# Query projection in two 64-row halves, runs of four or eight heads at a time, in a fused attention and MLP kernel

## The chip, the cores and the metric

The kernel runs on one core of one Trainium2 chip. The metric is the device time of one execution in microseconds (us), given as the median of several runs with its lowest and highest. Profiles are single executions; their span is a few us off the median, which matters only where it is said.

## The reference, cut to what matters

```python
xn = layernorm(x)                                    # S=2048 rows, D=576 columns, bf16
# A: attention over the last W=512 keys of the cache, 32 query heads, 16 key heads, Dh=128
q = (xn @ wq).reshape(1, S, 32, 128)                 # wq: 576 x 4096
k, v = last W keys of k_cache, v_cache, each repeated for two query heads
s = (softmax(q @ k.T * Dh**-0.5) @ v).reshape(1, S, 4096) @ wo
# B: an MLP block of the same input
h  = gelu(layernorm(xn) @ w1)                        # 576 x 576
hs = (quarters of h shifted by +1, -1, +2, -2 rows) @ w2
x1 = xn + hs
g  = silu(x1 + gelu(layernorm(x1) @ w3) @ w4)        # inner width 4608
out = x + s * g
```

## The kernel before

The 2048 rows are four blocks of 512 (numbered 0 to 3). A block goes through 32 attention *units*, one per head. A unit is: the q projection of the next head, four score matmuls (one per 128 keys) each followed by an exp on ACT, and the sixteen output matmuls of the head before, whose result DVE divides by the softmax sums into a buffer `o`; SP then transposes `o` by DMA. Work of other stages (the first half of B, the product with wo of the block before) is put between these as filler. Block 0 also has to load and transpose all keys and load V, wq, w1 and wo.

```python
P, QB, NDC = 128, 512, 5            # 576 = 4 * 128 + 64: five passes, the last one half zeros
ps_sc = pool("ps_sc", 3, PSUM)      # score banks
ps_pq = pool("ps_pq", 2, PSUM)      # q banks
ps_po = pool("ps_po", 2, PSUM)      # output banks
o_pool = pool("o_pool", 4)

def load_wq(j, eng=None):                      # weights of four heads
    ...
    eng.dma_start(out=w[:, 0:NF, :], in_=A_wq[0:NF * P, ...])
    eng.dma_start(out=w[0:DR, NF, :], in_=A_wq[NF * P:D, ...])      # the 64 rows left

def late(ap, fn):                              # a load that may start only once `ap` is there
    g = nc.gpsimd.tensor_copy(out=gate[:, :], in_=ap)
    with tc.issue_after(g.ins):
        fn()

def stage_q(u):
    ...
    psq = ps_pq.tile([P, QB], FP32, name="psq", tag="pq")
    for kc in range(NDC):
        nc.tensor.matmul(psq[:, :], lhsT=w[:, kc, hh * Dh:(hh + 1) * Dh], rhs=xT_b[qb % 2][:, kc, :],
                         start=(kc == 0), stop=(kc == NDC - 1))
    ...                                        # DVE (block 0) or ACT copies psq to qT

def stage_v(u, t0):                            # two of the four row tiles of a head
    ...
    with tc.high_priority(offset=HP):
        nc.vector.reciprocal(out=ri, in_=po[:, :, Dh])
        nc.vector.tensor_tensor(out=o[:, t0:t0 + 2, :], in0=po[:, :, 0:Dh], in1=..., op=ALU.mult)

def stage_t(u):
    oT_t[u] = oT = oT_pool.tile([P, TB, P], BF16, name="oT")
    nc.sync.dma_start(out=oT[:], in_=o_t.pop(u)[:].rearrange("p a b -> p (a b)"), transpose=True)

# loads of block 0, by unit                    (all of these on the POOL queue)
at(2, lambda: late(pT_t[2]..., load_w1))
for i in range(8):
    at(4 + 3 * i, lambda i=i: late(pT_t[4 + 3 * i]..., lambda: load_wo(i)))
...
with tc.manual_schedule(engines={SP, POOL, PE}):   # DVE and ACT are ordered by priority
    for u in ...:
        for i in range(4):
            stage_s(u, i)
            if i == 0:
                stage_q(u + 1)                     # one head's q in every unit
            elif i < 3:
                stage_v(u - 1, 2 * (i - 1))
            ...                                    # a third of the unit's filler
        stage_t(u - 1)
```

## Time and profile before

| | |
|---|---|
| median of 3 runs | 853.12 us (850.93 to 855.52) |
| span of the profiled run | 847.5 us |
| from the first exp to block 1 (block 0) | 103.1 us |
| blocks 1, 2, 3 | 133.7, 134.3, 136.8 us |
| product with wo of block 3, then the MLP | 32.9 us, then 293.7 us |

A stage time here runs from the first exp of a block to the first exp of the next, read from the trace.

The second view is the last line of the transposed outputs' own view, the time from the issue of a transpose to its landing:

```profile
DMA to landing us min/median/max: 2.4/3.2/9.8
```

### The profile page before, as it was taken

How to read it: one execution, taken by the hardware profiler on the slowest of the kernel's cores; microseconds unless marked ns; L12 is line 12 of the kernel's file. 1: busy time of each engine (PE TensorE's matmuls, PEld its weight loads, DVE VectorE, ACT ScalarE, POOL GpSimd, SP SyncE). 2: the span in 40 equal slices, each digit the busy share in tenths (PEclk: the TensorE clock that was granted, in tenths of full speed). 3: DMA queues.
4: the chain of work that ended last, by engine and by line, in shares of the span. 5: the costliest groups of instructions: out<-in, count | busy, mean ns of one | idle time of the engine just before them, and what ended most of it. 6: DMA issues, size and time to landing. Idle time of an engine off the chain costs nothing.

```text
span 847.5 us, 19375 instructions
## 1 busy us (share of the span) xinstructions
PE 826.8 (98%) x7896; PEld 485.0 (57%) x7980; DVE 427.7 (50%) x1351; ACT 460.9 (54%) x825; POOL 76.9 (9%) x134
## 2 busy tenths in 40 slices
PE   8999899999999999999999999999999999999996
PEld 5665555665564565565566565455555555555555
DVE  5778841267751166762154884052247537635324
ACT  5776763598793388784379874132333333334610
POOL 3441200310010111010001100000000000000000
PEclk9999999999999999999999999999999999999999
DMA  7996751473372174363048336992003301310101
GB/s 181 234 234 159 157 97 41 117 125 91 87 136 43 41 130 99 91 126 82 19 82 164 70 79 105 307 342 47 2 2 74 99 2 43 69 64 15 44 15 46
DMA packets 139983, 83.94 MB, mean 99 GB/s; under 512 B 106944, under 2 KB 133248, under 8 KB 139888
## 3 DMA queue, kind: packets, MB, share of 16 engines
q1 hardware_dynamic: 130048, 53.01, 30.6%
q0 software_dynamic: 8448, 28.15, 11.8%
q10 hardware_dynamic: 1392, 1.48, 0.5%
q8 instruction: 64, 1.05, 0.5%
q14 instruction: 31, 0.25, 0.1%
HBM read 49.17 MB, written 9.44 MB: 69 GB/s over the span
## 4 chain that ended last, share of the span: by engine, by line

## 5 line engine op out<-in xcount | busy, mean ns | idle before, releaser
L367 ACT ACTIVATE pT<-sc 128x512 bf16<-128x512 f32 x512 | 290.3, 596 | 103.5 <-PE sc L365 91.4
L365 PE MATMUL sc<-qT,kT 128*128 128x512 bf16 x493 | 175.1, 378 | 1.3 <-DVE qT L355 0.6
L382 PEld LDWEIGHTS <-pT 128*128 128x128 bf16 x2048 | 139.5, 98 | 52.9 <-DVE o L387 2.5
L382 PE MATMUL po<-v_sb,pT 128*128 128x129 bf16 x2048 | 161.4, 220 | 3.2 <-DVE o L387 2.0
L350 PE MATMUL psq<-xT_b,wq_b 128*128 128x512 bf16 x603 | 151.9, 379 | 2.5 <-DMA xT_b<-xn_b 0.4
L386 DVE RECIPROCAL ri_b<-po 128x2 f32<-128x2 f32 x256 | 43.0, 168 | 189.3 <-PE po L382 185.3
L731 PE MATMUL ph<-xT_b,w_s 64*128 64x512 bf16 x976 | 127.1, 376 | 2.3 <-DVE fence L721 2.1
L768 PE MATMUL pm<-w_s,h 64*128 64x512 bf16 x864 | 122.2, 377 | 0.9 <-DVE fence L721 0.9
L406 PE MATMUL pswo<-wo_sb,oT 128*128 128x512 bf16 x497 | 114.2, 379 | 0.8
L387 DVE TENSOR_TENSOR o<-po,ri_b 128x256 bf16<-128x256 f32 x256 | 107.9, 422 | 10.7 <-DMA oT<-o 4.3
L749 ACT ACTIVATE h<-ph 128x512 bf16<-128x512 f32 x67 | 39.4, 597 | 133.9 <-PE ph L731 133.9
L350 PEld LDWEIGHTS <-wq_b 128*128 128x128 bf16 x640 | 62.4, 98 | 74.4 <-issue 2.2
L768 PEld LDWEIGHTS <-h 64*128 64x128 bf16 x1728 | 70.8, 94 | 56.7 <-issue 1.6
L406 PEld LDWEIGHTS <-oT 128*128 128x128 bf16 x1024 | 64.9, 98 | 55.2
L768 PE MATMUL pr<-w_s,h 64*128 64x64 bf16 x864 | 90.2, 189 | 0.2 <-ACT h L749 0.2
L731 PEld LDWEIGHTS <-w_s 64*128 64x128 bf16 x1152 | 57.3, 94 | 51.0 <-issue 2.8
L357 ACT ACTIVATE qT<-psq 128x512 bf16<-128x512 f32 x96 | 57.4, 598 | 28.1 <-PE psq L350 26.7
L747 DVE COPY hx<-ph 128x512 f32<-128x512 f32 x55 | 38.0, 692 | 67.8 <-PE ph L731 67.8
L365 PEld LDWEIGHTS <-kT 128*128 128x128 bf16 x512 | 47.4, 97 | 28.4 <-DVE qT L355 1.2
L227 POOL DMA_DIRECT2D wq_b<-in_A_wq_dram x30 | 23.4, 780 | 314.4 <-PE psq L350 295.4
L721 DVE TENSOR_SCALAR fence<-ph,ph 1x1 f32<-1x1 f32 x61 | 12.6, 206 | 53.9 <-PE ph L731 53.4
L749 ACT ACTIVATE h<-hx 128x512 bf16<-128x512 f32 x55 | 34.6, 630 | 8.5 <-DVE hx L747 7.0
(114 smaller groups left out, 641.3 us busy)
## 6 DMA issues: line engine op xcount, KB each, us to landing
wq_b<-in_A_wq_dram POOLq DMA_DIRECT2D x30, 512.0 KB, 5.3
w_s<-in_B_w_dram SPq DMA_DIRECT2D x9, 576.0 KB, 7.0
wo_sb<-in_A_wo_dram POOLq DMA_DIRECT2D x8, 576.0 KB, 5.0
w_s<-in_B_w_dram SPq DMA_DIRECT2D x9, 512.0 KB, 7.9
x_dram<-x SPq DMA_DIRECT2D x4, 576.0 KB, 3.5
x<-x_dram SPq DMA_DIRECT2D x4, 576.0 KB, 5.1
s_b<-s_dram SPq DMA_DIRECT2D x4, 576.0 KB, 5.4
x_b<-in_A_x_dram SPq DMA_DIRECT2D x4, 576.0 KB, 6.6
```

Of the source, the lines that this page charges most:

```text
L350: nc.tensor.matmul(psq[:, :], lhsT=w[:, kc, hh * Dh:(hh + 1) * Dh], rhs=xT_b[qb % 2][:, kc, :], start=(kc == 0), stop=(kc == NDC - 1))
L357: nc.scalar.activation(out=qT[:, :], in_=psq[:, :], func=ACT.Copy)
L365: nc.tensor.matmul(sc[:, :], lhsT=kT[:, g, kc * P:(kc + 1) * P], rhs=qT_t[u][:, :], start=True, stop=True)
L367: nc.scalar.activation(out=pT[:, :], in_=sc[:, :], func=ACT.Exp, scale=SCALE)
L382: nc.tensor.matmul(po[:, j, :], lhsT=pTs[kc][:, tt * P:(tt + 1) * P], rhs=v_sb[:, g, kc, 0:Dh + 1], start=(kc == 0), stop=(kc == KCH - 1))
L386: nc.vector.reciprocal(out=ri, in_=po[:, :, Dh])
L387: nc.vector.tensor_tensor(out=o[:, t0:t0 + 2, :], in0=po[:, :, 0:Dh], in1=ri.unsqueeze(2).to_broadcast([P, 2, Dh]), op=ALU.mult)
L406: nc.tensor.matmul(ps, lhsT=oT_t[qb * Hq + h][:, tt, :], rhs=wo_sb[:, h, lo:hi], start=(h == 0), stop=(h == Hq - 1))
L731: nc.tensor.matmul(ps[i][:, :], lhsT=lhsT, rhs=xT[half, kc, :], start=first, stop=last, skip_group_check=True)
L747: nc.vector.tensor_copy(out=src[:, :], in_=ps[i][:, :])
L749: nc.scalar.activation(out=h3[:, :], in_=src[:, :], func=ACT.Gelu_apprx_tanh)
L768: nc.tensor.matmul(out, lhsT=h3_t[b, fc][half, tt * P:(tt + 1) * P], rhs=w4_s[fc // WS][half, fc % WS, lo:hi], start=key not in started, s ...
```

## The change

The intent is to take the zeros out of q. A 64-row PE tile does half the rows of a matmul, and two such tiles, the upper and the lower half of the array, work side by side. For two heads the 576 rows are 18 half passes in 9 slots instead of 10 full passes. Since changing between full and half tiles costs time (some 0.2 us there and back in these traces), four heads (in block 0) or eight (in blocks 1 to 3) are done in one run. That needs banks: a run borrows score and output banks, chosen by who needs them next. DVE and ACT now run in a hand-made order, in which layernorm and gelu come as small pieces, each with an estimated time, placed when a credit of TensorE time has built up. Block 0's weight loads are moved to other units.

```diff
+        def stage_qs(u0, n):
+            ...
+            X, Y, Z = (ps_pq, "pq"), (ps_po, "po"), (ps_sc, "sc")
+            banks = [X, Y] if u0 == 0 else [Z, X] if n == 4 else [X, Y, Z, X]
+            for u2 in range(u0, u0 + n, 4):
+                for u in (u2, u2 + 2):
+                    ps = [... two banks ...]
+                    q_half(xT, u, ps, [(kc, ((0, LO), (1, HI))) for kc in range(NDC)], True)
+                    nc.vector.tensor_scalar(out=f[:, :], in0=ps[0][0:1, 0:1], scalar1=ps[1][0:1, 0:1], ...)  # fence
+                for u, ps in pairs:
+                    q_half(xT, u, ps, [(kc, ((1, LO), (0, HI))) for kc in range(NF)], False)
+                    nc.scalar.activation(out=qT_t[u][:, :], in_=ps[0][:, :], func=ACT.Copy)
+                    nc.vector.tensor_copy(out=qT_t[u + 1][:, :], in_=ps[1][:, :])
+        def quarter(us):                        # called after each quarter of a unit
+            clock["credit"] = min(clock["credit"] + us, 1.2)
+            while clock["credit"] > 0.25:       # put one more small piece on DVE
+                ...
@@ load_wq: the tail rows go to both halves of the array
-            eng.dma_start(out=w[0:DR, NF, :], in_=A_wq[NF * P:D, c0:c0 + 4 * Dh])
+            for half in (LO, HI):
+                eng.dma_start(out=w[half, NF, :], in_=A_wq[NF * P:D, c0:c0 + 4 * Dh])
@@ pools and loads
-        o_pool = pool("o_pool", 4)
+        o_pool = pool("o_pool", 5)
-        at(2, lambda: late(pT_t[2][0][0:1, 0:1], load_w1))
+        at(13, lambda: late(pT_t[13][0][0:1, 0:1], load_w1))
-            at(4 + 3 * i, lambda i=i: late(pT_t[4 + 3 * i][0][0:1, 0:1], lambda: load_wo(i)))
+            at(9 + 3 * i, lambda i=i: late(pT_t[9 + 3 * i][0][0:1, 0:1], lambda: load_wo(i)))
-            at(4 * (j - 1) - 1, lambda j=j: load_wq(j))
+            at(4 * (j - 2) + 1 if j < 10 else 8 * (j // 2 - 1) + 1 + j % 2, lambda j=j: load_wq(j))
@@ the order; us is the TensorE time that an atom of filler is said to take
-        def pe(u, atoms):
+        def pe(u, atoms, us=0.216):
-                pe(o2 + 3, b2_rem(bb))
+                pe(u + 3, b2_rem(bb))
-        with tc.manual_schedule(engines={SP, POOL, PE}):
+        with tc.manual_schedule(engines={SP, POOL, PE, DVE, ACTE}):
+                if u % (4 if u < Hq else 8) == 0 and 0 < u < U:
+                    stage_qs(u, 4 if u < Hq else 8)
-                        if u + 1 < U:
-                            stage_q(u + 1)
@@ also: Newton's inverse square root in four steps instead of one; layernorm's tail
@@ columns written twice; x loaded straight into the layernorm buffer; (cut)
```

## The prediction

> **What bounds the kernel now.** I read the page first, then busy time by stretch, then what TensorE waited for, then single units of the attention loop in order of time. The page's first section says who is full:
>
> ```profile
> PE 826.8 (98%) x7896; PEld 485.0 (57%) x7980; DVE 427.7 (50%) x1351; ACT 460.9 (54%) x825; POOL 76.9 (9%) x134
> ```
>
> By stretch (attention block 0, then block 1, then the start of the MLP; columns are length, then busy us and count of each engine):
>
> ```profile
> 12.50:113.50 101.00, 97.88 (x829) 61.26 (x845) 79.23 (x256) 73.53 (x131) 30.90 (x52) 1.00 0.85 180
> 113.50:248.00 134.50, 133.44 (x1110) 79.74 (x1129) 65.19 (x225) 92.76 (x172) 17.40 (x30) 1.00 0.45 97
> ...
> 554.00:660.00 106.00, 103.69 (x1296) 56.90 (x1294) 50.50 (x153) 37.04 (x61) 0.00 (x0) 1.00 0.32 84
> ```
>
> TensorE (first number after the length) is full in every stage. Block 0 is where ACT (fourth, 73.5 of 101) and DVE (third, 79.2) come nearest to it and the DMA engines are busy 0.85 of the time. So a change pays only where it shortens TensorE's own instruction stream or removes one of its waits. The waits, one list before 554 us and one after it (total us, times, longest):
>
> ```profile
> PE po L382 <- DVE o L387: 2.0, 1, 2.0
> ...
> PE ph L731 <- DVE fence L721: 2.1, 2, 1.0
> PE pm L768 <- DVE fence L721: 0.9, 1, 0.9
> ```
>
> The first is at 103 us: an attention output waits in DVE for a buffer that a slow DMA transpose holds. The other three sit in the MLP at 567, 648 and 720 us. At each, DVE is in the middle of the eleven small operations of one Newton inverse square root, 0.2 us apart, all ahead of the fence that TensorE needs. Together the waits of any size are only some 7 us; the rest of the time is instructions.
>
> One attention unit (one head of one block) without filler work, in order of time:
>
> ```profile
> 108.66 0.38 PE L365 MATMUL sc<-qT,kT 128*128 128x512 bf16 x1
> 108.88 0.63 PE L382 MATMUL po<-v_sb,pT 128*128 128x129 bf16 x8
> 109.34 0.59 PE L365 MATMUL sc<-qT,kT 128*128 128x512 bf16 x2
> 109.99 1.03 PE L350 MATMUL psq<-xT_b,wq_b 128*128 128x512 bf16 x4
> 110.85 0.38 PE L365 MATMUL sc<-qT,kT 128*128 128x512 bf16 x1
> 111.07 0.63 PE L382 MATMUL po<-v_sb,pT 128*128 128x129 bf16 x8
> 111.54 0.38 PE L365 MATMUL sc<-qT,kT 128*128 128x512 bf16 x1
> ```
>
> Start to start, a 512-column matmul costs 0.216 us (110.85 to 111.07; its 0.38 is latency) and eight 129-column ones 0.47 (0.059 each). The unit takes 111.54 - 108.66 = 2.88 us = 4 scores x 0.216 + 5 q x 0.216 (one q record is missing from the trace) + 16 x 0.059. The q projection is 1.08 of it: 576 rows done as five passes of 128, the last half zeros.
>
> **What the Trainium skill says.** "TensorE: Matmul & The Clock Gate", section "Wait — 56ns, not 53.3ns?", gives 215.7 ns start to start for 512 columns at full clock; the trace agrees (0.216). "TensorEngine Tiling (Array Packing)", section "Key Properties": two 64-row tiles work in parallel, but changing the tiling mode drains TensorE; and its "Gotcha 1: PSUM Pressure" says that different row tiles must not write one PSUM bank at once and software has to see to it, which is what the fences are for. The MLP of the kernel before already runs this way and shows both the rate and the drain:
>
> ```profile
> 551.81 2.03 PE L406 MATMUL pswr<-wo_sb,oT 128*128 128x64 bf16 x64
> 553.77 1.04 PE L731 MATMUL ph<-xT_b,w_s 64*128 64x512 bf16 x8
> 554.65 0.38 PE L731 MATMUL ph<-xT_b,w3r_s 64*128 64x512 bf16 x2
> 554.86 0.81 PE L731 MATMUL pr<-xT_b,w_s 64*128 64x512 bf16 x6
> ```
> ```profile
> 804.45 1.04 PE L731 MATMUL ph<-xT_b,w_s 64*128 64x512 bf16 x8
> 805.43 0.39 PE L931 MATMUL pm<-w_s,h 128*128 128x512 bf16 x1
> ```
>
> A pair of 64-row matmuls takes the slot of one (554.65 to 554.86). Into the mode: the last 64-column matmul starts at 551.81 + 2.03 - 0.19 = 553.65 and the next comes 0.12 later instead of 0.03, so 0.10 lost (0.01 more on the first slot). Out of it: the last pair starts at 804.45 + 1.04 - 0.38 = 805.11 and the next comes after 0.32 instead of 0.20, so 0.12 (0.01 more). A round trip is about 0.23 us. "ScalarE: Activation LUTs", section "What ACT_TABLE_LOAD costs", says that back-to-back ACTIVATEs overlap by about 93 ns; here an exp of 0.597 us is followed after 0.48 to 0.50 at the shortest, so rather more overlap:
>
> ```profile
> 299.18 0.60 ACT L357 ACTIVATE qT<-psq 128x512 bf16<-128x512 f32 x1 [0.27 <-PE psq L350]
> 299.68 2.17 ACT L367 ACTIVATE pT<-sc 128x512 bf16<-128x512 f32 x4
> ```
>
> **The change, part by part.**
> 1. Two heads' q are 18 half-height matmuls in 9 slots instead of 10 full ones: 64 pairs x 1 slot x 0.216 = **-13.8 us**, all of it on TensorE's path. The order of the instructions confirms the count: 1152 half matmuls for 640.
> 2. Mode changes: block 0 has 8 runs of four, blocks 1 to 3 have 4 runs of eight each, so 20 round trips x 0.23 = **+4.6**. The 64 new fences on DVE are 0.2 us each and lie beside the next pair's 1.08 us.
> 3. Layernorm and Newton steps become single small pieces placed by hand. In the MLP a fence then has at most three operations (0.6 us) ahead of it, not eleven (2.2): of the 3.0 us of fence waits I take **-2.8**.
> 4. Five o buffers for four, and block 0's w1 and wo loads moved later and further apart: the 2.0 us wait at 103 us goes, and with it a 0.5 us wait for the transposed x near 380: **-2.5**.
> 5. Start: layernorm writes the 64 tail columns twice (four small operations, 0.7 us), but four q in a row hide the 0.56 us that TensorE waited for its first q copy: **+0.3**.
> 6. New waits. Without q in it a unit is 4 x 0.216 + 16 x 0.059 = 1.81 us on TensorE, while ACT needs 4 x 0.478 = 1.91. Some 60 units of blocks 1 to 3 have no filler, so ACT falls behind by 0.1 each; three score banks take up an estimated 0.4 us a run before TensorE must wait: **+2**. In block 0 a run of four starts in two of the three score banks; the second of them was written by the third score of the unit before, whose exp ends about 1.0 us after that score starts, while TensorE gets there after 0.9 (later if ACT lags). Seven runs x 0.2 = **+1.5**. An output bank now has to be emptied within 0.9 to 1.1 us (two quarters of a unit), and DVE's latency for it is 0.17 + 0.2 + 0.42 = 0.8 with nothing in between: **+1** for the times when a layernorm piece is in between.
>
> Sum: -13.8 + 4.6 - 2.8 - 2.5 + 0.3 + 4.5 = **-9.7 us**.
>
> **Rivals.** (a) *ACT becomes the bound*: during 7.8 us of eight q it has three exps and four copies and then idles, then must do 32 exps at 0.478 = 15.3 where TensorE offers 14.5. Speaks for it: block 0's numbers above. Against: units with wo, w1 or w2 filler give ACT its slack back, and ACT is busy only 69% of block 1. If the banks absorb nothing it costs 6 us and not 2: about 847. (b) *DVE's hand-made order stalls TensorE*: it is the first time DVE and ACT run in strict program order in attention; a layernorm piece ahead of a fence, a q copy or an output would hold TensorE. DVE is near 80% full in block 0. If each of the 20 runs loses 0.3 more: 849. (c) *The waits vanish altogether*: all of part 6 near zero gives 839. (d) *DMA transposes of o take over*: landings of 5 to 10 us between 21 and 63 us against o buffers that at 1.91 us a unit come round in some 10 us; a few waits of 1 to 2 us, 847.
>
> **Range and chances.** 853.1 - 9.7 = 843.4 us. (c) sets the low end, 837; (a), (b) or (d) the high end, 849. Faster by over 2% means under 836: more than parts 1 to 4 give with no new wait but a microsecond, 0.1. Slower by over 2% would need 27 us of new waits in a stream that is full now, 0.02. Within 2%: 0.88.
>
> **What would show it.** In the page of the changed kernel: q pairs 0.216 apart in runs of 36 slots (part 1); about 0.1 us between the last full-height matmul and the first half-height one, and again at the end (2); no fence wait of 1 us in the MLP (3); no DMA behind a TensorE wait at 103 us (4); TensorE waits named after exps or score banks, small and in filler-free units, and q in block 0 waiting for ACT (6). Wrong would make it: a drain longer than the 0.1 us of a stream at its end, half-height pairs slower than 0.216 because 18 weight loads replace 10, or DVE waits above 5 us in attention.

## More of the kernel before

The prediction shows the lines for the bound, the waits and one unit. Two more views are needed later. The first is busy time by stretch, for two 5 us stretches of block 0: length, then busy us and count of PE, PEld, DVE, ACT and POOL, then the granted TensorE clock, the busy share of the DMA engines and the GB/s that they moved.

```profile
50.00:55.00 5.00, 4.99 (x44) 3.19 (x44) 3.39 (x11) 4.09 (x8) 1.48 (x3) 1.00 1.20 240
55.00:60.00 5.00, 4.95 (x51) 3.37 (x50) 3.52 (x10) 3.61 (x7) 1.29 (x2) 1.00 1.41 221
```

TensorE is full. The DMA share is above 1, since the times of packets are summed and those of an engine overlap, and over 200 GB/s are delivered.

## The result, and the profile after

The changed kernel took **885.06 us** (883.86 to 899.34, 4 runs, one of them slow), against 852.02 us (849.35 to 855.52) of the kernel before on the same chip. The ratio is **1.038 [1.033, 1.043]**: slower. Ratios here are the mean time of one kernel's fast runs over that of the other's of the same rounds, so they are not quite the ratio of the medians quoted beside them. Executions over 1.5% slower than the fastest of the same kernel are left out of the means.

The stages of the two profiled runs, in us:

| | start | block 0 | block 1 | block 2 | block 3 | wo of block 3 | MLP to the end | span |
|---|---|---|---|---|---|---|---|---|
| before | 12.9 | 103.1 | 133.7 | 134.3 | 136.8 | 32.9 | 293.7 | 847.5 |
| after | 16.9 | 123.7 | 146.4 | 135.7 | 136.7 | 33.4 | 290.8 | 883.6 |
| change | +4.0 | +20.6 | +12.7 | +1.4 | -0.1 | +0.5 | -2.9 | +36.1 |

First the page's line of busy time, then busy time by stretch of the kernel after (columns as above; blocks 0, 1 and 3, and the MLP from its first to its last big matmul).

```profile
PE 836.9 (95%) x8439; PEld 487.6 (55%) x8492; DVE 476.5 (54%) x1463; ACT 430.9 (49%) x793; POOL 90.8 (10%) x161
...
```

```profile
16.50:140.50 124.00, 104.64 (x1001) 63.62 (x1010) 73.64 (x248) 76.19 (x150) 36.86 (x64) 0.96 0.89 159
140.50:287.00 146.50, 140.01 (x1255) 82.14 (x1265) 95.38 (x307) 84.28 (x158) 21.46 (x39) 0.98 0.40 96
...
422.50:559.50 137.00, 131.18 (x1205) 78.32 (x1216) 75.53 (x235) 79.95 (x151) 9.15 (x15) 0.99 0.36 77
...
592.50:840.50 248.00, 247.85 (x3038) 136.28 (x3034) 122.64 (x341) 96.11 (x162) 1.08 (x1) 1.00 0.32 86
```

TensorE's share fell from 98% to 95%, although its busy time rose by 10 us. In block 0 it is busy 104.6 of 124.0 us, and the clock there is 0.96, so waiting has also cost clock. The MLP is as full as before, and shorter. What TensorE waited for in block 0 (total us, times, longest), then the same for DVE:

```profile
PE po L461 <- DVE o L468: 13.7, 7, 6.1
PE ph L543 <- issue: 3.2, 1, 3.2
```

```profile
DVE o L468 <- DMA oT<-o: 20.1, 8, 6.0
```

An output matmul waits for a bank; the bank waits for DVE; DVE waits for an `o` buffer, and the buffer for the DMA transpose that reads it. It is the wait that the prediction had seen for 2.0 us, now 13.7. The 3.2 us has the same root: the transposes of the layernormed block, which the w1 product needs, go through the same SP queue; the last of them landed at 116.7 us, and the product started at 116.8. The SP queue's order of time (start, length), and the transposes' landing times:

```profile
54.34 21.61 SPq L478 DMA_TRANSPOSE oT<-o  x6
76.00 2.74 SPq L322 DMA_TRANSPOSE xT_b<-xn_b  x1
```

```profile
DMA to landing us min/median/max: 2.4/2.6/24.3
```

The row of six runs from the first start to the last end; between two of them SP also waits for `o`. Its own issue times in it are 1.19, 2.22, 1.33, 2.70, 2.80 and 6.65 us, where 1.19 is the median over the kernel. Nine transposes, those of the layernormed blocks included, land after more than 10 us (none before). Two stretches of that time:

```profile
75.00:80.00 5.00, 0.00 (x0) 0.00 (x0) 0.29 (x1) 0.00 (x0) 2.29 (x3) 0.73 1.28 110
85.00:90.00 5.00, 4.21 (x42) 2.35 (x40) 4.19 (x16) 2.60 (x6) 0.00 (x0) 1.00 0.99 51
```

This is the line to remember: the DMA engines are about as busy as before (1.28, then 0.99, against 1.20 and 1.41) but deliver 110 and then 51 GB/s, not 221 to 240. TensorE does nothing for 5 us. Just ahead of this stretch the POOL queue, which issues the loads, shows:

```profile
54.38 0.80 POOL L297 DMA_DIRECT2D wo_sb<-in_A_wo_dram  x1 [0.31 <-issue]
55.16 0.77 POOL L245 DMA_DIRECT2D x<-in_A_k_cache_dram  x1
55.92 1.48 POOL L251 DMA_DIRECT2D v_sb<-in_A_v_cache_dram  x2
...
57.51 0.75 POOL L301 DMA_DIRECT2D w_sb<-in_B_w_dram  x1
...
58.79 0.78 POOL L233 DMA_DIRECT2D wq_b<-in_A_wq_dram  x1
```

A group of wo, keys of four heads, two V, w1 and wq start within 4.4 us; by 68 us a second wo and another V follow, some 3.5 MB by their shapes. Units without q last 1.9 us instead of 2.9, so, as I read it, loads placed unit by unit now come in bursts.

The idle time is followed by half clock. The trace has stretches at 0.5 from 77.3 us (6.8 us long), 97.7 (3.4), 247.9 (6.8) and 527.8 (3.4); the kernel before has only its very end. The Trainium skill, "TensorE: Matmul & The Clock Gate", section "What's actually happening", gives a free-running window of about 3.4 us after which an idle array loses half its clock; the lengths of 3.4 and 6.8 us agree.

Not everything failed. The start of a run of four q, in order of time:

```profile
36.23 4.33 PE L436 MATMUL psq<-xT_b,wq_b 64*128 64x512 bf16 x36
40.49 0.39 PE L444 MATMUL sc<-qT,kT 128*128 128x512 bf16 x1
```

From 36.23 to 40.49 are 4.26 us: 18 slots of 0.216 are 3.89, and leaving the mode costs about 0.1 (entering it cost 0.10 just before 36.23). The other 0.27 is a wait for a score bank: the run's second half matmul starts 0.29 us after the first, and the two halves stay one step apart to the end. e10 below supports this: there exps are shorter, so banks come free sooner, and the same run takes 3.99 us. Half-height pairs run at the predicted rate.

Block 1 loses its time elsewhere. DVE from 244.22 us on, in order of time (start, length), and TensorE beside it:

```profile
244.22 1.44 DVE L149 TENSOR_SCALAR xn_b<-xn_b,ln_mv,nr_y 128x64 bf16<-128x64 bf16 x4
245.58 0.16 DVE L467 RECIPROCAL ri_b<-po 128x2 f32<-128x2 f32 x1
245.78 0.42 DVE L468 TENSOR_TENSOR o<-po,ri_b 128x256 bf16<-128x256 f32 x1
246.12 0.41 DVE L626 TENSOR_TENSOR x<-psx1r,xn_b 128x256 bf16<-128x256 f32 x1
246.45 1.43 DVE L149 TENSOR_SCALAR xn_b<-xn_b,ln_mv,nr_y 128x64 bf16<-128x64 bf16 x4
```

```profile
246.26 0.41 PE L461 MATMUL po<-v_sb,pT 128*128 128x129 bf16 x4 [1.99 <-DVE o L468]
```

DVE emptied an output bank (245.78) only after four layernorm pieces (244.22), and TensorE stood 1.99 us. A pile of layernorm pieces just there is not chance: `b2_rem`, the last 20 matmuls of the w2 product with 64 columns each, is entered in the hand-made order at the default of 0.216 us per matmul, 4.3 us, and takes 0.029 us each, 0.6 us. The order believes in 3.7 us of TensorE time that does not exist and fills them with DVE work. Then:

```profile
248.00:254.00 6.00, 5.17 (x31) 3.52 (x32) 3.51 (x14) 2.99 (x6) 0.00 (x0) 0.50 0.75 172
```

### The profile page after: what moved, and what is told of

Its sections match the earlier page's. It is cut to its first block, busy times and chain, and to the rows that moved or that the text cites. A ratio compares the mean times of both kernels' runs of the same rounds, so it can differ in the third digit from the quotient of the medians.

```text
span 883.6 us, 20509 instructions
## 1 busy us (share of the span) xinstructions
PE 836.9 (95%) x8439; PEld 487.6 (55%) x8492; DVE 476.5 (54%) x1463; ACT 430.9 (49%) x793; POOL 90.8 (10%) x161
## 4 chain that ended last, share of the span: by engine, by line
## 5 line engine op out<-in xcount | busy, mean ns | idle before, releaser
L446 ACT ACTIVATE pT<-sc 128x512 bf16<-128x512 f32 x512 | 268.8, 669 | 113.9 <-PE sc L444 110.6
L461 PE MATMUL po<-v_sb,pT 128*128 128x129 bf16 x2048 | 206.1, 223 | 24.5 <-DVE o L468 21.9
L461 PEld LDWEIGHTS <-pT 128*128 128x128 bf16 x2048 | 159.8, 99 | 100.8 <-DVE o L468 27.8
L444 PE MATMUL sc<-qT,kT 128*128 128x512 bf16 x489 | 187.9, 384 | 1.7 <-ACT pT L446 1.3
L436 PE MATMUL psq<-xT_b,wq_b 64*128 64x512 bf16 x1152 | 131.4, 380 | 1.4 <-DVE fence L420 0.7
L489 PE MATMUL pswo<-wo_sb,oT 128*128 128x512 bf16 x497 | 117.0, 379 | 1.3 <-ACT x L499 0.5
L467 DVE RECIPROCAL ri_b<-po 128x2 f32<-128x2 f32 x256 | 42.7, 167 | 116.8 <-PE po L461 107.9
L436 PEld LDWEIGHTS <-wq_b 64*128 64x128 bf16 x1152 | 56.8, 95 | 68.9 <-issue 5.7
L428 ACT ACTIVATE qT<-psq 128x512 bf16<-128x512 f32 x64 | 38.2, 597 | 90.7 <-PE psq L436 90.7
L444 PEld LDWEIGHTS <-kT 128*128 128x128 bf16 x512 | 50.6, 99 | 20.7 <-issue 8.5
L429 DVE CAST qT<-psq 128x512 bf16<-128x512 f32 x64 | 44.2, 690 | 19.0 <-PE psq L436 18.8
```

Of the source, the lines that this page charges most:

```text
L428: nc.scalar.activation(out=qT_t[u][:, :], in_=ps[0][:, :], func=ACT.Copy)
L429: nc.vector.tensor_copy(out=qT_t[u + 1][:, :], in_=ps[1][:, :])
L436: nc.tensor.matmul(ps[k][:, :], lhsT=w[half, kc, hh * Dh:(hh + 1) * Dh], rhs=xT[half, kc, :], start=(first and kc == 0), stop=(not first a ...
L444: nc.tensor.matmul(sc[:, :], lhsT=kT[:, g, kc * P:(kc + 1) * P], rhs=qT_t[u][:, :], start=True, stop=True)
L446: nc.scalar.activation(out=pT[:, :], in_=sc[:, :], func=ACT.Exp, scale=SCALE)
L461: nc.tensor.matmul(po[:, j, :], lhsT=pTs[kc][:, tt * P:(tt + 1) * P], rhs=v_sb[:, g, kc, 0:Dh + 1], start=(kc == 0), stop=(kc == KCH - 1))
```

## The experiments

All kernels were checked against the reference's outputs on the chip and reported correct within its tolerance. e3, e6, e7 and e10 compute a wrong result, with the reference's shapes (parts of the weights or of the outputs replaced or not loaded); the tolerance does not see it. The kernel before ran beside each group: 858.77 us (849.63 to 867.76) beside e1 to e4, on a noisier chip (two of its 7 runs slow), 852.91 (850.47 to 858.32) beside e5 to e8, and 852.3 (851.01 to 866.33, three runs slow) beside e9 to e12. Stage times in the text are from each profile.

### e1, e2: the position of the loads

The first theory (A) was the later w1 and wo loads: they fall into the last half of block 0. e1 moves w1 back, e2 both.

```diff
-        at(13, lambda: late(pT_t[13][0][0:1, 0:1], load_w1))
+        at(2, lambda: late(pT_t[2][0][0:1, 0:1], load_w1))
-            at(9 + 3 * i, lambda i=i: late(pT_t[9 + 3 * i]..., lambda: load_wo(i)))      # e2 only
+            at(4 + 3 * i, lambda i=i: late(pT_t[4 + 3 * i]..., lambda: load_wo(i)))
```

> The changed kernel with one edit: block 0's load of w1 goes back from unit 13 to unit 2. Theory A (the burst of wo, K, V, w1 and wq loads that starts at unit 12 swamps the DMA engines, DMA transposes of o then land after 15 to 24 us and the five o buffers run out): the landings fall back under 10 us, the TensorE waits for DVE's o in block 0 fall from 13.5 us to under 4, and the time falls by 12 to 25 us, to 860 to 873. Rival B (block 0 is slow because units without q are 1.9 us long and the transposes cannot follow them, whatever is loaded): w1 makes little difference, 878 to 887.

> The changed kernel with w1 at unit 2 and wo at units 4, 7, 10 and so on, as the kernel before has them. Theory A: about like the first run of this call or up to 5 us better, 857 to 870. Rival B: 878 to 887. If this is clearly slower than the first run, the later wo loads of the change are right by themselves and only w1 is misplaced.

e1: 880.08 us (875.77 to 887.04), ratio 1.030 [1.019, 1.040]; block 0 119.3 us against 123.7, waits for `o` 8.4 us and not under 4, landings up to 16.5 us. e2: 898.58 (892.71 to 900.18), ratio 1.051 [1.043, 1.059]; block 0 132.3, with 14 transposes over 10 us. With w1 alone moved back the gain is within the scatter of block 0 (see e3), and 880.08 lies in rival B's range; with both old positions it is worse. Theory A falls. Rival B falls later: e6 and e8 have the same short units and a block 0 of 106 to 108 us.

### e3: the number of small loads

```diff
-            for half in (LO, HI):
+            for half in (LO, HI) if j < 2 else (LO,):
```

> The changed kernel without the second load of the 64 tail rows of wq after the first two (stale rows: a wrong result on purpose), 30 of 90 weight DMAs on the POOL queue fewer. Theory A counts bytes and sees only 64 KB less per four heads, under a tenth: time stays over 875. Rival C (the number of small DMAs on that queue is what slows it): block 0 recovers, 858 to 870.

880.84 us (878.89 to 882.46), ratio 1.030 [1.022, 1.038]; block 0 116.4, seven transposes over 10 us. That is 7.3 us less, but e5 below, which changes nothing in block 0, has 120.8, so some of it is scatter. The second tail load of each wq is a small part at most; without it most of the loss is still there.

### e4: Newton's steps split, alone, in the kernel before

```diff
+        def inv_part(k): ...                    # begin, then three Newton steps, each its own piece
-            return [lambda i=i: step(i) for i in range(2 * TB + 1)] + [lambda: ln3_transpose(b)]
+            return [lambda i=i: step(i) for i in range(2 * TB + 4)] + [lambda: ln3_transpose(b)]
```

> The kernel before with one part of the change alone: in the MLP the Newton inverse square root is cut into four small pieces. The three fence waits of 1 us there should go, and nothing else changes: 3 us faster than the kernel before, ratio 0.9965 (0.994 to 0.999). If the 4.0 us that the MLP gained in the changed kernel came from elsewhere, the ratio is 1.000.

853.22 us (849.18 to 853.44), ratio 0.996 [0.988, 1.004]. From the first big matmul of the MLP to its last 251.7 us became 247.8, the same as in the changed kernel (247.7). So part 3 of the change is worth 4 us in the MLP's stage, and needs nothing of the rest. Yet the total did not move beyond the noise: block 0 of this run took 110.4 us instead of 103.1, with six transposes over 10 us, although nothing of block 0 was changed. The kernel before is itself at the edge of the same trouble.

### e5: the cost of the w2 remainder

```diff
-                pe(u + 3, b2_rem(bb))
+                pe(u + 3, b2_rem(bb), 0.029)
```

> The changed kernel, one number of its hand-made order put right: the 20 matmuls of 64 columns in the remainder of the w2 product are entered at their 0.029 us and not at 0.216. Theory: as it stands the order believes in 3.7 us of TensorE time that do not exist and puts as much layernorm work into DVE ahead of the outputs; blocks 1 and 3 should each lose 3 to 4 us of TensorE waits for DVE's o (3.5 and 3.7 in the changed kernel), so block 1 about 142.5 and block 3 about 133, block 0 as it was. Rival: the waits come from the scarcity of output banks whatever the order; they stay within 1 us.

885.37 us (873.15 to 886.6, 5 runs), ratio 1.039 [1.033, 1.044]: in the total no faster than the changed kernel. The profiled run, the fastest, took 873.15 us, with block 1 at 139.9 (146.4 after), block 2 at 135.3 and block 3 at 132.4 (136.7 after). That is 6.5, 0.4 and 4.3 less, more than the 3 to 4 expected for blocks 1 and 3. Block 1's list has no wait for `o` any more (3.5 us in the changed kernel), and the half clock in blocks 1 and 3 went with the waits. The four other runs were 882.47 to 886.6, 9 us and more longer. That block 0 differs between runs would explain it, and their granted clock, 0.980 to 0.985 against 0.988, fits longer waits; but these runs have no profile, so this is argued and not shown. The blocks' times carry the verdict on the mechanism; e9 gives it a steady total.

### e6: an eighth of the wo bytes in block 0

wo is loaded once (4 heads) and used for all; a wrong result.

```diff
         def load_wo(i):
+            if i:
+                return
```

> The changed kernel with one of eight wo loads (every head uses the first four heads' wo: a wrong result on purpose): 4.1 MB less to load in block 0 and nothing else changed. Theory A2 (the sum of loads and DMA transposes of block 0 is more than the DMA engines carry, whatever the order): block 0 falls from 124 to 98 to 104 us, no transpose lands after 10 us. Rival B (TensorE's and DVE's order in block 0 is the cause): block 0 stays over 115.

866.9 us (866.61 to 868.38), ratio 1.017 [1.012, 1.022]; block 0 106.0, the slowest transpose 13.5 us. Fewer loads help by 18 us, though neither expectation is met: block 0 is just above the 98 to 104 of A2, and six transposes land after more than 10 us. It does not tell bytes from the number of loads under way.

### e7: half the transposes in block 0

```diff
         def stage_t(u):
+            if u < Hq and u % 2:
+                oT_t[u] = oT_t[u - 1]
+                return
```

> The changed kernel with every second DMA transpose of o in block 0 left out (its neighbour's result is used: a wrong result on purpose); all loads stay. Theory A2: block 0 falls to 98 to 106 us, as in the run without wo loads. If the loads alone are the matter (loads pile up by themselves), the loads still land after 12 us and more, but with half the transposes behind them TensorE waits less: 108 to 116.

886.1 us (884.36 to 889.17), ratio 1.039 [1.033, 1.045]; block 0 125.0. Half the transposes, and no gain: block 0 lies above both expected ranges. So the transposes are more victims than cause, and the loads pile up without them; nine of those left still land after more than 10 us. TensorE's waits in block 0 of this run:

```profile
PE po L461 <- DVE o L468: 13.1, 2, 12.9
```

### e8: the same loads, two or three at a time

Before each load of block 0 POOL touches a value of the load before the last, so that it can be issued only when that has landed. No byte less is loaded.

```diff
+        def pace(ap):
+            if len(recent) > 1:
+                nc.gpsimd.tensor_copy(out=gate[:, :], in_=recent[-2])
+            recent.append(ap)
         def load_wq(j, eng=None): ...
+            pace(w[0:1, 0, 0:1])                # POOL, block 0 only; the same in load_k, load_v, load_wo, load_w1
```

> The changed kernel with the same loads, but in block 0 a weight load is issued only when the load before the last has landed, so that two or three are under way and not eight. Theory A3 (it is not the bytes but up to eight loads outstanding at once, in front of which each transpose queues on every DMA engine): transposes land within 10 us, block 0 falls to 100 to 108, time to 862 to 870. If the bytes are too many (A2) pacing only moves the wait to the weights: block 0 stays over 112.

871.47 us (869.98 to 873.16), ratio 1.022 [1.017, 1.028]; block 0 107.6 us, 16.1 less. Its waits of TensorE in block 0, then the landing line:

```profile
PE psq L450 <- ACT pT L460: 2.7, 1, 2.7
PE po L475 <- DVE o L482: 1.0, 2, 0.8
```

```profile
DMA to landing us min/median/max: 2.4/2.6/9.9
```

The wait for `o` went from 13.7 to 1.0 us. (With the transposes of the layernormed blocks, the slowest landing is 10.1 us.) The wait of 2.7 us is new, and it is the pacing's own. ACT in that stretch:

```profile
63.71 1.09 ACT L460 ACTIVATE pT<-sc 128x512 bf16<-128x512 f32 x2 [2.65 <-POOL gate L285]
```

ACT could not write its next `pT` until POOL, held up by the pacing, had read an old one at the gate in `late`. The table gives, for 5 us each, the mean number of loads between issue and landing, and the GB/s of all DMA, worked out from the traces' DMA records:

```
from us          55         60         65         70         75
before        2.9 221    3.7 208    2.1 247    1.0  45    4.3 296
after         4.6 247    7.8 105    7.8 240    7.9 192    7.2 110
e4            3.4 217    4.4  99    4.2 216    2.6 132    0.3  56
e6            4.9 211    6.6 203    7.4 155    5.7 156    3.1 105
e7            4.5 229    7.7 253    7.8 185    7.1 236    4.6  90
e8            1.7 156    2.1 223    3.6 265    2.8 201    3.4 205
```

The before kernel has at most 5.5 (at 40 us), e8 at most 3.8. Of the runs in the table, only those with long landings have seven to eight loads under way, e7 with half the transposes among them. But this number is no threshold: the changed kernel still moved 240 GB/s with 7.8, and e4, whose means stay under 6, moved 99 with 4.4 and had six landings over 10 us. What e8 shows is that the bytes alone (A2) are not the cause: it has those of the changed kernel and loses the long waits. It alters two things that go together, the number under way and the moment at which each load starts, and cannot tell them apart. Why many loads under way make the engines slow, rather than only the queue long, no run here shows.

### e9: e8 and e5 together

> Both repairs together: loads paced (never more than two or three under way in block 0) and the remainder's matmuls entered at 0.029 us. If they act on separate causes their gains add: block 0 about 107, block 1 about 140, block 3 about 132, span about 883.6 - 16 - 11 = 857, still 8 to 10 us slower than the kernel before. If the order of DVE was only slow because of the DMA (or the other way round), the sum is under 22 us: over 861.

857.73 us (857.16 to 858.52), ratio 1.005 [0.999, 1.011], and the times are narrow. Blocks 105.0, 139.8, 135.3, 132.4; the MLP 290.9; no transpose over 8.9 us. The repairs add up in the blocks' times (883.6 - 16.1 - 11.2 = 856.3 against a span of 855.6), and the ratio goes from 1.038 to 1.022 with e8 and to 1.005 with both; e5 alone had not shown in the ratio (1.039). A stretch of block 0 again:

```profile
80.00:85.00 5.00, 4.95 (x54) 3.23 (x52) 4.18 (x14) 4.20 (x9) 2.60 (x5) 1.00 1.35 209
```

TensorE is full and 209 GB/s arrive at a DMA share of 1.35. With both faults mended, the change still gains nothing against the kernel before. By stages of the two profiles the span is 8.1 us longer: start +5.8, block 0 +1.9, blocks 1 to 3 +2.7, wo of block 3 +0.5, MLP -2.8. Of this, 2.7 us are the pacing's own wait, and 1.6 us come from the first q run, which took 5.68 us, partly at half clock (12.0 to 15.5 us), and 4.06 in the changed kernel's profile. Without these two the span would be some 851 us, an estimate from these numbers: still no gain.

### e10: a faster ACT, as a probe

e9 with exps over three of the four row tiles (384 columns, not 512), the output matmuls of the fourth tile reading the third; a wrong result.

```diff
-            nc.scalar.activation(out=pT[:, :], in_=sc[:, :], func=ACT.Exp, scale=SCALE)
+            nc.scalar.activation(out=pT[:, 0:3 * P], in_=sc[:, 0:3 * P], func=ACT.Exp, scale=SCALE)
```

> The repaired kernel with each exp over 384 columns and not 512 (a wrong result on purpose), which leaves TensorE's work as it is. Theory: in units without q ACT's 0.478 us an exp is the pace and TensorE waits for score banks (2.6, 2.1 and 1.4 us of small waits ahead of a score in blocks 1 to 3): these fall under 0.3 us a block, and blocks 1 to 3 together are 5 to 8 us shorter than in the repaired kernel. Rival: the small waits are weight loads or mode changes of TensorE itself; then the blocks stay within 1.5 us.

849.78 us (847.3 to 851.13), ratio 0.995 [0.988, 1.001]. Blocks 1 to 3 went from 407.5 to 401.9 us, 5.6 less. In e9 a score after an output matmul started more than 12 ns late 43, 52 and 35 times in blocks 1, 2 and 3, by 2.6, 2.1 and 1.4 us in all; in e10 these sums are 0.14, 0.04 and 0.03. ACT's pace does cost 5 to 6 us of blocks 1 to 3, more than the prediction's 2. In block 0 five runs of four went from 4.27 to 3.99 us, so ACT also costs 0.28 at each of these.

### e11: runs of four in all blocks

e9 with shorter runs, which let ACT catch up more often.

```diff
-                if u % (4 if u < Hq else 8) == 0 and 0 < u < U:
-                    stage_qs(u, 4 if u < Hq else 8)
+                if u % 4 == 0 and 0 < u < U:
+                    stage_qs(u, 4)
```

> The repaired kernel with q in runs of four in every block. Eight at a time is there to save mode changes: 12 more round trips x 0.23 = 2.8 us more. If ACT's lag grows with the number of units since the last run, runs of four give back up to 5 us of score bank waits, and the sum is 0 to 3 us faster; if not, it is 2 to 5 us slower.

872.87 us (868.45 to 875.05), ratio 1.021 [1.014, 1.029]; blocks 1 to 3 146.5, 143.3, 138.3. The experiment does not answer its question: the wq loads stand where runs of eight need them, and runs of four use them earlier, so TensorE waited five times for wq, 8.1 us in all, longest 2.9. Inconclusive on ACT.

### e12: what of the change helps the kernel before

The kernel before with the split Newton steps of e4 and the pacing of e8.

> The kernel before with the two things that this study found good: Newton in four pieces in the MLP (-3.7 us in its profile) and block 0's loads paced. Its block 0 took 103 us in one profile and 110 in another, where six transposes landed after 10 us; if paced loads keep it at 101 to 104, it is 3 to 8 us faster than the kernel before, ratio 0.990 to 0.997, and faster than both kernels. If pacing only delays loads that the kernel before needs, the ratio is over 0.998.

848.54 us (847.22 to 853.51, 6 runs), ratio 0.995 [0.989, 1.000]; block 0 105.7, above the 101 to 104 expected (one 2.9 us wait is left there), no transpose over 8.2 us, the first to the last big matmul of the MLP as in e4. It is the best correct version and faster than both kernels by median, but the interval just reaches even, well within 2%. Since e4 alone has 0.996, a share of the pacing in it is not shown.

## Why the prediction was wrong, point by point

It said 843.4 us, between 837 and 849, with 0.88 for no change beyond 2%; the result is 885.06. By its own steps:

**Step 1 (fewer slots, -13.8) and step 2 (mode changes, +4.6): right.** Half matmuls come at 0.216 a pair, and a round trip costs about 0.21 (0.10 in; out, the undelayed runs of e10, 3.99 us, are 0.11 over 18 slots). The gain did come into TensorE's stream: worked out from the instructions of the four blocks by their slot times, it needs 487.2 us after against 504.2 before, and 2.8 of the 17.0 are q that moved into the start, so 14.2 less.

**Step 3 (Newton, -2.8): right, a little small.** No fence wait is left between 600 and 845 us; the stretch fell by 4.0 us, and by 3.9 in e4 alone.

**Step 4 ("the 2.0 us wait at 103 us goes": -2.5): this is the step that failed most.** It counted buffers and spread the loads by unit numbers, and did not ask how long those units would be. (The wait near 380 us that it put at 0.5 us is 0.4 in its list.) Instead of -2.5 block 0 took 25.5 us more than its stream of 96.4 + 1.8 for mode changes. Of it 18.6 are listed waits (13.7 for `o`, 3.2 for the w1 product's input, the rest small), and about 3.5 are half clock while TensorE worked (7.0 of the 10.2 us at half clock). e8 removes 16.1 of the 25.5 with the bytes unchanged, so most of it comes from loads that are issued without waiting for earlier ones; e1, e2, e3 and e7 rule out where in the order the loads stand, their small tails and the number of transposes as the main cause. Rival (d) named the mechanism, DMA transposes holding `o`, but sized it "a few waits of 1 to 2 us": the sizes came from the landings of the kernel before, and the change altered those landings themselves.

**Step 5 (start, +0.3): too small.** The start is 4.0 us longer. Three more q are done there, 2.8 us that was in block 0 before; 1.2 are left.

**Step 6 (new waits, +4.5): its first and third terms were too small.** The first (ACT falls behind, +2) measures 5.6 in e10; by the prediction's own numbers, 60 units at 0.1 less 0.4 in each of 12 runs, it was 1.2. The second (score banks at a run of four in block 0, +1.5) was about right: 0.28 in each of the four undisturbed runs of the changed kernel, and five such runs in e9 make 1.4, which e10 takes away. The third (output banks, +1) was right in naming a layernorm piece ahead of an output, but took it as chance. It was built in by the wrong cost of the w2 remainder: e5 takes 6.5, 0.4 and 4.3 us from the three blocks, so 11 us with the half clock that followed.

**What no step had.** e9 has both faults repaired, and its blocks 1 to 3 still take 407.5 us for a stream of 390.8 (before: 404.8 for 404.5). Of the 16.7 us above the stream, mode changes are about 2.4 (11 in these blocks, worked out) and ACT's pace is 5.6 (e10). Between 8 and 9 remain. Some 4.6 of them are still on e10's list of waits, and the list of the kernel before has none of the kind in these blocks: 1.9 for the sum bank of w2, 1.4 for DVE's `o`, 1.0 for the banks of the wo product, 0.3 at a q run; no run took them away one by one, so this split stays open. Its block 0 takes 105.0 for 98.2, with the pacing's 2.7 us in it. So the gain in the stream was real and was used up. That the kernel before hides these waits behind the q of each unit fits the lists, but no run shows it alone.

**Rivals (a), (b), (c).** ACT as a bound (a) was the right idea at 5.6 us against its 6. (b) said that the hand-made order would lose up to 6 us; it lost 11, by one wrong number. (c), that all waits vanish, is not seen anywhere. **What would make it wrong** named "DVE waits above 5 us in attention", which is what came (21.9 us for DVE's `o` in all).

The change of the span, +36.1, adds up, but for rounding, as: start +4.0, block 0 +20.6, blocks 1 to 3 +14.0, wo of block 3 +0.5, MLP -2.9.

## What to carry to other kernels

When a full engine's stream gets shorter, every latency beside it is to be counted again: loads placed by step number come closer together, buffers are wanted sooner, ACT's pace counts. Watch how long transfers take to land and what they deliver, not the DMA engines' busy share, which read 1.2 to 1.4 at 240 GB/s and at 110. A hand-made order is only as good as each cost entered in it, and one wrong number in a list cost 11 us; and try each part alone, since here the one part that shortened its stage as hoped, by 4 us in the MLP, needed none of the others.

## What the Trainium skill lacked or had wrong

- "TensorEngine Tiling (Array Packing)", section "Key Properties", says that a mode change drains TensorE and gives no figure. Here it costs about 0.10 us into 64-row tiles and 0.11 to 0.12 out of them: 0.23 a round trip in the kernel before, about 0.21 in the changed one.
- "TensorE: Matmul & The Clock Gate", section "Back-to-back issue gap", has sustained matmuls of 512 columns about 131 ns apart. Every stream here, of full matmuls or of half-height pairs, comes at 0.216 us, which is the figure of the same page's "Wait — 56ns, not 53.3ns?".
- The same page, section "Why this matters for your kernels", warns of idle gaps over about 3 us. Here two shorter waits, 2.0 us and, 1.1 us of work later, 1.5 us, were enough for 6.8 us at half clock, from 247.9 us, within the second wait.
- "ScalarE: Activation LUTs", section "What ACT_TABLE_LOAD costs", gives an overlap of about 93 ns for ACTIVATEs in a row. An exp of 0.597 us is followed after 0.478 here, so 119 ns.
- "DMA: Bandwidth & Descriptors", section "Rules for kernel authors", says that a transpose next to ordinary DMAs needs nothing. That may hold for its result; for its time it does not: transposes of `o`, which in the kernel before landed after 2.4 us at least and 9.8 at most, took up to 24.3 us in the changed kernel, and at most 9.9 us again with the loads paced (e8). No page has a figure for this.
